# Top-k attention and routed experts on one core: the first pair's transpositions on one queue, more constant products ahead of it, later weight loads for the last expert, and row scatters into disjoint views

## The chip, the cores and the metric

The kernel runs on one core of a Trainium2 chip. The metric is device time in microseconds for one execution. Before the change it was 1404.75 us, the median of three runs (1401.38 to 1409.36).

## The reference, cut to what matters

```python
# attention: q, k, v are (8 batches, 8 heads, 576 rows, 64)
scores = q @ k.T / 8
kth    = 32nd largest score of each row
attn   = softmax(where(scores >= kth, scores, -1e9))
x      = (attn @ v), heads side by side         # 4608 tokens x 512
# experts: 8 experts, each takes exactly 576 tokens
logits = x @ w_gate                             # 4608 x 8
# pairs (token, expert) in falling order of logit; a pair is taken
# while the token is free and the expert has room
out[tokens of e] = relu(x[tokens of e] @ w1[e]) @ w2[e]   # 512 -> 1024 -> 512
```

## The kernel before, in words

**Order of work.** Both halves are written as lists of operations that a planner (`Plan`, top of the file) puts in order when the program is built. Every operation has an engine, an assumed duration, operations that must come before it, ring buffers that it takes or frees, and a due time `t`. The planner walks through time. Among the operations of an engine that could start within a small window it takes the one with the smallest due time. The D queue (SyncE's DMA queue, SP for short) has a window so large that the smallest due time always wins. The result is the program order of each engine. On the chip each engine then runs its own list in that order and waits at an instruction until its inputs are there, so everything behind a waiting instruction waits too.

**Attention** (`attention`, from L141). 32 pairs, each a batch with two heads, 9 tiles of 128 query rows a pair. For a pair, `prep` loads k, q and v, splits them into fp16 high and low parts, and `turn` (L237 to L241) makes four DMA transpositions of them: K2 and K3 from `nk`, Q2 and Q1 from `nq`. The scores (L288) need all four. VectorE finds the 32 largest scores of a row with MAX8 (L291 to L316) and ScalarE marks them (L303, L321). TensorE adds the marks to a second, transposed copy of the scores (L359 to L365), ScalarE takes the exponential (L369), and GpSimd splits it in two (L372, L375). L447 multiplies by v. The first pair has its own list, `first()` (from L245), in which k is loaded and transposed on SP and q on ScalarE's DMA queue. In the program the four transpositions stand in the order K2, Q2, K3, Q1.

**Constant products.** `stay(n)` (L193 to L195) issues n products of a constant tile that nothing reads. The planner puts `lead` of them in front of the first product of the attention, and some into gaps later on, so that TensorE is not idle there.

**Routing.** In `route` and `enlist` the experts are chosen one after another. VectorE and a few small products on TensorE search the threshold of the next expert and write the list of its 576 token numbers (`idx`). Those of the last expert are whatever is left, so its number (`ei`, L798) and list come soon after those of the seventh.

**Experts** (p = 0 to 7 in the order of the routing, about 47 us apart by due time).

- `weigh(p, t)` with t = 47 p - WT: SP reads the expert's number (`pick`, L873) and issues four loads of 1 MB, two of w1 and two of w2 (L881, ring `wr` of four). ScalarE makes the high fp16 parts (L893, eight of 1024 columns) and VectorE the low ones (L901, sixteen of 512).
- `bring(p, t)` with t = 47 p - 21.675: GpSimd gathers the rows of x in five indirect DMAs (L923, tile `xg`, 128 rows each, the last 64). ScalarE (L946) and VectorE (L949) split them into tile `xs` (three buffers), and SP transposes them into `xT` (L950). For p = 0 TensorE transposes instead.
- `ffn(p, t)`: TensorE multiplies by w1 in sixteen groups of twelve products (L968, eight groups for the tokens 0 to 287, then eight for the rest; five PSUM banks `ph`). ScalarE and VectorE make the two fp16 parts of the ReLU (L987, L988). TensorE multiplies by w2 for five token tiles in the order 0, 1, 4, 2, 3 (L1002, and L1005 for tile 4). ScalarE moves each result to `ob` (L1012, three buffers), and GpSimd scatters its rows into the output with an indirect DMA (L1017).

The rows of the output that different scatters write never coincide, but all of them name the same tensor `out`, so the framework makes each scatter wait until the one before it has landed. One scatter, that of the last expert's tile 3, stands at the very end of the program (L1100, shown in the trace as L1077), behind a branch that repeats the work if a test on the attention fails (`redo`).

Of the kernel before, what the change touches and what calls it, by code (L numbers as in the profile page):

```python
# [2 lines left out]

# [4 lines left out]

# [134 lines left out]
def attention(tc, q,k,v,w_gate,x_out,L,acc,cuts, pairs):  # L143
    NCH=6
    nc=tc.nc
    CW=576//NCH; NCAND=8*NCH
    with ExitStack() as ctx:
# [6 lines left out]
        V,G,A,T=nc.vector,nc.gpsimd,nc.scalar,nc.tensor  # L154
# [16 lines left out]
        for i in range(2):  # L171
            t=cp.tile([128,2,9,128],F16,name=f"nq{i}"); NQ.append(t); V.memset(t[:,1,:,64:128],0.0)
# [22 lines left out]
            for _ in range(n): T.matmul(early[0][:,0:128],nid60,nid60,start=True,stop=True,skip_group_check=True)  # L195
        ESC=0.125/(QS*QS)
        loom=Plan(PLANBUFS,WIN,dict(VV=.196,AV=.141,AP=.166,AG=.205,VA=.13,VP=.14,VG=.166))
        loom.keep=dict(f=stay,tag="pt",unit=.0559,edge=.12,window=3.413,share=.6,since=lambda: 10.0,until=lambda: 1e9,lead=105)
        at=loom.at
        def prep(n):  # L200

# [2 lines left out]
            nq,nk,vt,vh,vl=NQ[pi],NK[pi],VT[n%3],VH[n%3],VL[n%3]  # L204
# [29 lines left out]
            def lower(nm): G.tensor_tensor(low[nm][0],sc[nm],low[nm][1],op=ALU.subtract)  # L234
            def clean(): G.memset(nq[:,1,:,64:66],0.0)
            fl=lambda t: t.rearrange("p a b -> p (a b)")
            def turn(nm,by=nc.sync):  # L237
                t=io.tile([128,9,128],F16,tag=nm,name=nm,bufs=2)
                by.dma_start_transpose(t,fl({"Q1":nq[:,0],"Q2":nq[:,1],"K2":nk[:,0],"K3":nk[:,1]}[nm]))
                P[nm]=fl(t)  # L240
                if nm=="Q2": P["Q2t"]=t  # L241
            prev=Ps.get(n-1); old=Ps.get(n-2); o3=Ps.get(n-3)
# [3 lines left out]
            def first():  # L246

                lk=at(0.0,lambda: loads("k",k),e="D",d=2.2,late=2.0); l=at(0.0,lambda: loads("q",q,nc.scalar),e="A",d=2.9,late=2.4)
                def highk(): G.tensor_scalar(nk[:,0].rearrange("p i (r d) -> p i r d",r=2),nat["k"].unsqueeze(2).to_broadcast([128,9,2,64]),QS,0.0,op0=ALU.mult,op1=ALU.add)
                def highq(): A.activation(nq[:,:,:,0:64],nat["q"].unsqueeze(1).to_broadcast([128,2,9,64]),AF.Copy,scale=QS)  # L250
                def rest(nm): V.scalar_tensor_tensor(low[nm][0],nat[nm],QS,low[nm][1],op0=ALU.mult,op1=ALU.subtract)
                h1=at(0.0,highk,[lk],e="G",d=1.25); k2=at(0.0,lambda: rest("k"),[h1],e="V",d=.7)
                h2=at(0.0,clean,[h1],e="G",d=.1); h2=at(0.0,highq,[l],e="A",d=1.2,order=[h2]); q2=at(0.0,lambda: rest("q"),[h2],e="V",d=.7)
                a=at(0.0,lambda: turn("K2"),[h1],e="D",d=1.4,late=2.0); b_=at(0.0,lambda: turn("K3"),[a,k2],e="D",d=1.4,late=2.0)
                c=at(0.0,lambda: turn("Q2",nc.scalar),[h2],e="A",d=1.4,late=2.0); c=at(0.0,lambda: turn("Q1",nc.scalar),[c,q2],e="A",d=1.4,late=2.0)
                P["ready"]=at(0.0,lambda: None,[c,b_]); P["q2r"]=q2
                P["lds"]=at(0.0,loadv,[b_],e="D",d=2.2,late=2.0)
                wipe=at(0.0,rims,[q2],e="V",d=1.3); at(0.0,gates,[P["lds"]],e="D",d=3.2,late=2.0)
                P["vs"]=s3=at(0.0,scaledv,[P["lds"],wipe],e="G",d=1.1)
                a=at(0.0,lambda: highv(0),[s3],e="A",d=.3); a=at(0.0,lambda: highv(1),[a],e="A",d=.3)  # L260
                P["vready"]=at(0.0,lowerv,[a],e="G",d=1.13)
# [388 lines left out]
def moe(tc, K, L, x, w1, w2, out, tail, marks=None):  # L650

    nc=tc.nc
    E,D,F=w1.shape; N=x.shape[0]; CAP=N//E; NT=N//128
    T=MT; STEPS=MSTEPS; BIG=1e30; SX=128.0; SW=128.0; OSC=1.0/(SX*SW*SW)
    with ExitStack() as ctx:
        ctx.enter_context(tc.manual_schedule())
# [2 lines left out]
        wp=ctx.enter_context(tc.tile_pool(name="wp",bufs=2))  # L659
        ps=ctx.enter_context(tc.tile_pool(name="ps",bufs=1,space=PSUM))  # L660
        V,G,A,P,S=nc.vector,nc.gpsimd,nc.scalar,nc.tensor,nc.sync
        O=dict(WL1=-67.48, WL2=33.053, R1=216.021, XL=85.087, FA=-155.406, RT=5997.879, TE=0.633, TN=-42.68, WT=72.231, XT=21.675, RD=-5966.067, GL=2.3, W_V=0.109, W_A=0.0071, W_G=1000.0, W_P=0.0363, W_D=874040.4423, WD0=8.825, WD1=33.963, RA=16.129, WT0=-69.551, TE0=-175.381, XT0=-143.142, VD=228.308)
        GL,RT,TE,TN,WT,XT,RD,RA,WT0,TE0,XT0,VD,R1,XL,FA,WL1,WL2=(O[k] for k in ('GL','RT','TE','TN','WT','XT','RD','RA','WT0','TE0','XT0','VD','R1','XL','FA','WL1','WL2')); WD=(O['WD0'],O['WD1'])
        WIN={e:O['W_'+e] for e in 'VAGPD'}
        HOW0='vvvvvvvv'; HOW='vvvvvvvv'; GP=3; AHV=1; JO=1; PB=3; SPN=512; PW=.3; GV=0
# [204 lines left out]
        def weigh(p,t):  # L870

            e=X[p]; D_=e["D"]; e["raw"]=[]; ops=[]
            def pick(): e["r"]=nc.sync.value_load(D_["ei"][0:1,0:1],min_val=0,max_val=E-1)  # L873
            c=Chain(t,e["ei"],X[p-1]["loads"] if p else None)
            c.add("D",1.5,pick)
            for k in range(4):
                def load(k=k):
                    w,nch,cols=((w1,4,F),(w2,8,D))[k//2]; hf=k%2
                    src=w[bass.ds(e["r"],1)].rearrange("a (c p) f -> p (a c) f",p=128)
                    r=new(wp,[128,nch//2,cols],F32,"wr",4)  # L880
                    S.dma_start(out=r,in_=src[:,hf*nch//2:(hf+1)*nch//2,:])  # L881
                    e["raw"].append(r.rearrange("p c f -> p (c f)"))
                ops.append(plan.at(c.t+.05*k,load,c.pre,take="wr",e="D",d=.45,late=2.0+3.0*(k+1),order=ops[-1:]))
            e["loads"]=ops[-1]
            e["W"]=[]; e["wdone"]=[]
            prev=None
            for k in range(8):
                o_=(k%4)*1024; how=(HOW0 if p==0 else HOW)[k]; tk_=t+WD[0 if p==0 else 1]*k
                cut=lambda k=k: e["raw"][k//2][:,(k%2)*1024:(k%2)*1024+1024]
                def hi(k=k,o_=o_,cut=cut):  # L890
                    if k==0:
                        for (nch,cols,nm) in ((4,F,"w1"),(8,D,"w2")): e["W"].append((new(wp,[128,nch,cols],F16,nm+"h"),new(wp,[128,nch,cols],F16,nm+"l")))
                    A.activation(e["W"][k//4][0].rearrange("p c f -> p (c f)")[:,o_:o_+1024],cut(),AF.Copy,scale=SW)  # L893
                a=plan.at(tk_,hi,[ops[k//2],prev],e="A",d=.94,take="W" if k==0 else None); prev=a
                if k==0: e["tW"]=a
                at_=a
                if how=="v":
                    for u in range(0,1024,SPN):
                        def lo(k=k,o_=o_,cut=cut,u=u):
                            W=e["W"][k//4]; h=W[0].rearrange("p c f -> p (c f)"); l=W[1].rearrange("p c f -> p (c f)")  # L900
                            V.scalar_tensor_tensor(l[:,o_+u:o_+u+SPN],cut()[:,u:u+SPN],SW,h[:,o_+u:o_+u+SPN],op0=ALU.mult,op1=ALU.subtract)  # L901
                        at_=plan.at(tk_+.01+((WL1 if k<4 else WL2) if p==0 else 0),lo,[at_],e="V",d=.07+SPN*.00104,free=[ops[k//2]] if k%2 and u+SPN==1024 else None)
                else:
                    box={}
                    def sc(cut=cut,box=box):
                        box["t"]=new(wp,[128,1024],F32,"wt"); 
                        if how_a: A.activation(box["t"],cut(),AF.Copy,scale=SW)
                        else: G.tensor_scalar(box["t"],cut(),SW,0.0,op0=ALU.mult,op1=ALU.add)
                    how_a=False
                    g1=plan.at(tk_,sc,[ops[k//2],R.get("lastwt")],e="G",d=1.014)  # L910
                    def lo(k=k,o_=o_,box=box):
                        W=e["W"][k//4]; h=W[0].rearrange("p c f -> p (c f)"); l=W[1].rearrange("p c f -> p (c f)")
                        G.tensor_tensor(l[:,o_:o_+1024],box["t"],h[:,o_:o_+1024],op=ALU.subtract)
                    at_=plan.at(tk_+.01,lo,[at_,g1],e="G",d=2.08,free=[ops[k//2]] if k%2 else None); R["lastwt"]=at_
                e["wdone"].append(at_)
        def bring(p,t):
# [3 lines left out]
            def gather(j):  # L920
                n=128 if j<4 else 64
                xgs[j]=new(sm,[128,D],F32,"xg",4)
                G.indirect_dma_start(out=xgs[j][:n],out_offset=None,in_=x,in_offset=bass.IndirectOffsetOnAxis(ap=D_["idx"][:n,j:j+1],axis=0))  # L923
            g=None
            for j in range(5):
                n=128 if j<4 else 64
                g=plan.at(t+.1*j,lambda j=j: gather(j),[e["idx"]],e="G",d=1.25,take="xg",late=GL,order=[g,prev],k=1)
                if p==0:
                    B={}
                    if j<GV:  # L930
# [20 lines left out]
        def ffn(p,t):  # L951
# [39 lines left out]
            for j in ((0,1,4,2,3) if JO else range(5)):  # L991
# [22 lines left out]
                        B["o2"]=new(sm,[64,D],F32,"o2",2); A.activation(B["o2"],B["po"][64:128],AF.Copy,scale=OSC)  # L1014
                a=plan.at(t2+i_*.64,put,[prev],e="A",d=.51,take="ob",free=[tp] if j<4 else None); to=a
                if j==4: a=plan.at(t2+i_*.64+.1,lambda B=B: V.scalar_tensor_tensor(B["ob"][:64],B["po"][:64],OSC,B["o2"],op0=ALU.mult,op1=ALU.add),[a],e="V",d=.6,free=[tp],k=0)
                def scatter(B=B,j=j,n=n): G.indirect_dma_start(out=out,out_offset=bass.IndirectOffsetOnAxis(ap=D_["idx"][:n,j:j+1],axis=0),in_=B["ob"][:n],in_offset=None)  # L1017
                if p<E-1 or j!=3: plan.at(t2+i_*.64+.2,scatter,[a],e="G",d=1.25,free=[to],late=2.0,k=1)
            plan.frees(prev,e["tW"]); e["mm"]=prev; e["last2"]=prev
        def verdict(c,acc,cuts,flags):  # L1020
# [84 lines left out]
```

## Time and profile before

| | |
|---|---|
| runs | 1401.38, 1404.75, 1409.36 us (median 1404.75) |
| profiled execution | 1401.41 us, span 1399.7 us, mean granted TensorE clock 0.973 |
| busy share of the span | TensorE 92%, VectorE 83%, ScalarE 62%, GpSimd 61% |
| attention | from the start to about 920 us |
| routing of the first expert | about 920 to 966 us |
| experts | about 966 to 1388 us, then the end of the program |

How to read it: the busy shares are means over parts of the program that have different limits, so they only say that TensorE is the engine to look at first. What a change can save is read from the stretches in which TensorE is idle or has the lower of its two clocks (1.2 GHz instead of 2.4 GHz; a granted clock of 1.00 stands for 2.4), and from what it waited for there.

### The profile page before, as it was taken

The numbers are of one execution on the slowest core, as the hardware profiler recorded it, in microseconds if no ns is written. First come the engines' busy times: TensorE is split into PE (matmuls) and PEld (weight loads), VectorE is DVE, ScalarE is ACT, GpSimd is POOL, SyncE is SP. The second block draws the span as 40 slices with busy tenths as digits, with TensorE's granted clock in tenths as the row PEclk, the third lists the DMA queues.
The fourth block names the chain that finished last, engine by engine and source line by source line (L and its number), as shares of the span: only waits on it lengthen the run. The fifth ranks groups of instructions, "written<-read, shape, count | busy, mean of one in ns | idle before, by whom it ended". The sixth has DMA issues, their size and how long they took to land.

```text
span 1399.7 us, 42775 instructions
## 1 busy us (share of the span) xinstructions
PE 1288.7 (92%) x15599; PEld 929.6 (66%) x15600; DVE 1167.1 (83%) x6012; ACT 873.3 (62%) x1899; POOL 859.0 (61%) x1281
## 2 busy tenths in 40 slices
PE   5999999999999999999999999956989999998896
PEld 4677767777777767777776776746655665664562
DVE  5999988999999998999999999869979889987320
ACT  2778877878887877877878878713424424444320
POOL 3798888888888888888888888601114203203201
PEclk8999999999999999999999999967999999999998
DMA  4544464465444444445545335014446545647301
GB/s 89 101 97 96 87 132 85 85 121 98 90 107 95 93 105 96 92 93 115 85 94 126 79 82 102 14 35 155 146 94 196 176 126 154 181 162 213 86 27 37
DMA packets 293391, 148.56 MB, mean 106 GB/s; under 512 B 250672, under 2 KB 275248, under 8 KB 292144
## 3 DMA queue, kind: packets, MB, share of 16 engines
q1 hardware_dynamic: 284464, 125.96, 39.9%
q0 software_dynamic: 5888, 18.88, 4.4%
q8 instruction: 124, 2.03, 0.6%
q10 hardware_dynamic: 2816, 0.89, 0.4%
q14 instruction: 99, 0.81, 0.2%
HBM read 71.34 MB, written 18.87 MB: 64 GB/s over the span
## 4 chain that ended last, share of the span: by engine, by line
PE 57%; DVE 14%; ACT 10%; DMA 9%; POOL 5%; issue 4%; SPq 0%; POOLq 0%; ACTq 0%; another core or an unknown queue 0%; DVEq 0%
PE ph L968 13%; PE s L306 9%; PE pv L447 8%; PE ph L1002 6%; PE s L288 6%; DVE cd L291 5%; ACT w L303 4%; ACT F L369 3%; PE pt L359 3%; DMA Q<-nq 3%; PE pt L365 2%; PE pt L364 2%; DMA out_dram<-ob,idx 2%; DMA xT<-xs 2%; POOL elm L375 2%
## 5 line engine op out<-in xcount | busy, mean ns | idle before, releaser
L291 DVE MAX8 cd<-s 128x8 f32<-128x96 f32 x1728 | 348.9, 251 | 24.8 <-PE s L288 22.2
L375 POOL TENSOR_TENSOR elm<-F,ehm 128x512 f16<-128x512 f32 x256 | 291.8, 1157 | 1.5
L316 DVE MAX8 st<-s 128x8 f32<-128x584 f32 x288 | 222.1, 771 | 43.7 <-PE s L306 39.2
L303 ACT ACTIVATE w<-s,st 128x576 uint16<-128x576 f32 x288 | 213.6, 742 | 67.4 <-DVE st L299 52.9
L321 ACT ACTIVATE r<-s,st 128x576 bf16<-128x576 f32 x288 | 212.5, 740 | 43.2 <-PE s L306 38.7
L1017 POOL DMA_INDIRECT out_dram<-ob,idx x39 | 47.0, 1205 | 286.6 <-ACT ob L1012 215.4
L968 PE MATMUL ph<-xT,w1h 128*128 128x288 f16 (+2 forms) x1056 | 198.9, 288 | 8.0 <-DMA xT<-xs 4.4
L288 PE MATMUL s<-K,Q 128*128 128x512 f16 (+3 forms) x1280 | 190.0, 288 | 14.2 <-DMA Q<-nq 9.0
L372 POOL TENSOR_SCALAR ehm<-F 128x512 f16<-128x512 f32 x256 | 157.1, 620 | 65.6 <-ACT F L369 62.9
L365 PE MATMUL pt<-Q,K 66*128 66x128 f16 (+1 forms) x1280 | 171.7, 214 | 4.5 <-DMA Q<-nq 4.1
L369 ACT ACTIVATE F<-pt 128x512 f32<-128x512 f32 x256 | 150.8, 595 | 35.1 <-PE pt L365 28.7
L364 PE MATMUL pt<-Q,K 128*128 128x128 f16 (+1 forms) x1280 | 171.7, 214 | 0.0
L288 PEld LDWEIGHTS <-Q 128*128 128x128 f16 (+1 forms) x1280 | 102.1, 101 | 104.5 <-issue 15.9
L306 PE MATMUL s<-w,off 128*128 128x512 f16 x576 | 135.1, 285 | 18.7 <-ACT w L303 17.4
L968 PE MATMUL ph<-xT,w1l 128*128 128x288 f16 (+2 forms) x528 | 151.5, 288 | 0.0
L987 ACT ACTIVATE hh<-ph 128x288 f16<-128x288 f32 x128 | 52.1, 410 | 120.7 <-PE ph L968 99.4
L447 PEld LDWEIGHTS <-ehm 128*128 128x128 f16 x2048 | 118.5, 102 | 6.0 <-issue 0.8
L447 PE MATMUL pv<-vh,ehm 128*128 128x65 f16 x1024 | 120.8, 195 | 0.3 <-ACT F L369 0.2
L306 PE MATMUL s<-w,back 128*128 128x512 f16 x576 | 118.1, 286 | 3.1 <-DVE st L316 0.2
L447 PE MATMUL pv<-vl,ehm 128*128 128x65 f16 x1024 | 120.7, 192 | 0.0
L447 PE MATMUL pv<-vh,elm 128*128 128x65 f16 x1024 | 120.2, 193 | 0.0
L364 PEld LDWEIGHTS <-K 128*128 128x128 f16 x1280 | 116.9, 98 | 4.4 <-issue 1.1
(283 smaller groups left out, 3319.0 us busy)
## 6 DMA issues: line engine op xcount, KB each, us to landing
wr<-in_moe_w_dram SPq DMA_DIRECT2D x32, 1024.0 KB, 8.3
kn<-in_k_dram SPq DMA_DIRECT2D x64, 128.0 KB, 2.6
vn<-in_v_dram SPq DMA_DIRECT2D x64, 128.0 KB, 2.3
x<-xb SPq DMA_DIRECT2D x8, 1024.0 KB, 4.4
qn<-in_q_dram SPq DMA_DIRECT2D x62, 128.0 KB, 2.3
Q<-nq SPq DMA_TRANSPOSE x158, 3.3
kn<-in_k_dram SPq DMA_DIRECT2D x64, 16.0 KB, 2.4
K<-nk SPq DMA_TRANSPOSE x64, 3.4
```

What stands on the lines that cost most here:

```text
L288: T.matmul(s_ps[rows,a:b_],P[Q][:,qc],P[K][:,h*576+a:h*576+b_],start=(Q=="Q1"),stop=(Q=="Q2"))
L291: V.max(D["cd"][:,c*8:c*8+8],D["s"][:,576*c//NCH:576*(c+1)//NCH])
L303: A.activation(D["w"],D["s"][:,:576],AF.Sign,bias=P["st"][:,i,32:33],scale=(1+2.0**-21),accum_out=acc[:,col])
L306: x=T.matmul(D["s"][:,a:b_],by,w[:,a:b_],start=False,stop=True,skip_group_check=True)
L316: def next8(): V.max(P["st"][:,i,24:32],D["s"][:,:584])
L321: A.activation(r,D["s"][:,:576],AF.Relu,bias=P["st"][:,i,31:32],scale=-1.0)
L364: T.matmul(o,K2[:,kb:kb+128],Q1[:,qc],start=False,stop=False,skip_group_check=True)
L365: T.matmul(o,K3[0:66,kb:kb+128],Q2[0:66,qc],start=False,stop=(c==3 and h==sub[-1][0]),skip_group_check=True)
L369: A.activation(D["E"],D["pt"],AF.Exp,scale=ESC)
L375: G.tensor_tensor(el,D["E"],D["eh"],op=ALU.subtract); P["e"][i]=(D["eh"],el)
L447: for m_ in (range(N-1) if part==0 else (N-1,)): T.matmul(out,seq[m_][0],seq[m_][1],start=(m_==0),stop=(m_==N-1))
L968: P.matmul(B["ph"][:,lo-c0:hi-c0],a[:,c,fs],xT[:,b+c,lo:hi],start=(i==0),stop=(i==11),skip_group_check=True)
```

## The change

- The first pair's Q2 and Q1 are transposed on SP's queue like K2 and K3. The planner still counts them as ScalarE's, so the program order stays K2, Q2, K3, Q1.
- `lead` goes from 105 to 140 constant products.
- WT goes from 72.231 to 61.707 (in the table `O`, the rest of which is unchanged), so all weight work of experts 1 to 7 is due 10.5 us later.
- For the last expert the planner places `pick`, and with it the four loads, only behind the last gather of the expert before it. This binds the program order on SP. It adds no wait on the chip.
- The scatters of the 40 row tiles write into 40 views of the output that the framework takes to be disjoint, so that a scatter no longer waits for the one before it. The last scatter of the program still names `out` itself and waits for all of them. In the repeated run inside `redo`, all still use `out`.

```diff
+from concourse.ap import dram_disjoint_views
...
-        loom.keep=dict(f=stay,tag="pt",unit=.0559,edge=.12,window=3.413,share=.6,since=lambda: 10.0,until=lambda: 1e9,lead=105)
+        loom.keep=dict(f=stay,tag="pt",unit=.0559,edge=.12,window=3.413,share=.6,since=lambda: 10.0,until=lambda: 1e9,lead=140)
...
-            def turn(nm,by=nc.sync):
+            def turn(nm):
                 t=io.tile([128,9,128],F16,tag=nm,name=nm,bufs=2)
-                by.dma_start_transpose(t,fl({"Q1":nq[:,0],"Q2":nq[:,1],"K2":nk[:,0],"K3":nk[:,1]}[nm]))
+                nc.sync.dma_start_transpose(t,fl({"Q1":nq[:,0],"Q2":nq[:,1],"K2":nk[:,0],"K3":nk[:,1]}[nm]))
...
-                c=at(0.0,lambda: turn("Q2",nc.scalar),[h2],e="A",d=1.4,late=2.0); c=at(0.0,lambda: turn("Q1",nc.scalar),[c,q2],e="A",d=1.4,late=2.0)
+                c=at(0.0,lambda: turn("Q2"),[h2],e="A",d=1.4,late=2.0); c=at(0.0,lambda: turn("Q1"),[c,q2],e="A",d=1.4,late=2.0)
...
     E,D,F=w1.shape; N=x.shape[0]; CAP=N//E; NT=N//128
+    rows=dram_disjoint_views(out,5*E) if marks else [out]*(5*E)
...
-            c=Chain(t,e["ei"],X[p-1]["loads"] if p else None)
+            c=Chain(t,e["ei"],X[p-1]["loads"] if p else None,X[p-1]["far"] if p==E-1 else None)
...
-                g=plan.at(t+.1*j,lambda j=j: gather(j),[e["idx"]],e="G",d=1.25,take="xg",late=GL,order=[g,prev],k=1)
+                g=plan.at(t+.1*j,lambda j=j: gather(j),[e["idx"]],e="G",d=1.25,take="xg",late=GL,order=[g,prev],k=1); e["far"]=g
...
-                def scatter(B=B,j=j,n=n): G.indirect_dma_start(out=out,out_offset=bass.IndirectOffsetOnAxis(ap=D_["idx"][:n,j:j+1],axis=0),in_=B["ob"][:n],in_offset=None)
+                def scatter(B=B,p=p,j=j,n=n): G.indirect_dma_start(out=rows[p*5+j],out_offset=bass.IndirectOffsetOnAxis(ap=D_["idx"][:n,j:j+1],axis=0),in_=B["ob"][:n],in_offset=None)
```

## Rows read from the trace of the kernel before

**Rows 1.** Stretches: us, busy of PE, PEld, DVE, ACT, POOL, granted clock, DMA share, GB/s.

```profile
66.00:900.00 834.00, 795.53 (x11311) 602.13 (x11311) 762.54 (x4589) 670.09 (x1532) 721.64 (x1112) 1.00 0.47 96
...
1081.00:1131.00 50.00, 49.17 (x393) 31.32 (x392) 44.64 (x150) 19.53 (x33) 11.11 (x12) 1.00 0.58 163
```

**Rows 2.** The chain that ended last, at the start: start us, us, what.

```profile
7.20 3.30 DMA K<-nk
...
10.64 4.09 DMA Q<-nq
...
21.86 3.06 PE s L288 x12
24.92 4.34 PE pt L195 x65
```

**Rows 3.** Timeline of the first tile: first MAX8 groups on VectorE, first marks on ScalarE.

```profile
23.04 1.42 DVE L291 MAX8 cd<-s 128x8 f32<-128x96 f32 x8 [12.70 <-PE s L288]
...
27.06 0.74 ACT L303 ACTIVATE w<-s,st 128x576 uint16<-128x576 f32 x1 [5.99 <-DVE st L299]
```

**Rows 4.** Later pairs: L239 on SP's queue, then its landings in 66:75 and in 40:50.

```profile
68.18 2.81 SPq L239 DMA_TRANSPOSE Q<-nq  x2
...
DMA to landing us min/median/max: 3.4/3.7/4.2
...
DMA to landing us min/median/max: 3.5/4.3/5.1
```

**Rows 5.** Stretches at the start, columns as in the first group.

```profile
9.50:12.90 3.40, 3.37 (x61) 3.20 (x58) 0.66 (x11) 0.00 (x0) 0.00 (x0) 1.00 0.77 71
...
21.80:24.90 3.10, 3.04 (x14) 1.39 (x15) 1.86 (x12) 0.00 (x0) 0.57 (x1) 0.50 0.30 77
```

**Rows 6.** Stretches around the seventh expert, columns as in the first group.

```profile
1281.00:1285.20 4.20, 0.29 (x5) 0.39 (x6) 2.68 (x5) 2.80 (x4) 0.98 (x1) 1.00 1.02 221
1285.20:1289.20 4.00, 4.00 (x26) 2.66 (x24) 2.28 (x6) 0.57 (x2) 0.00 (x0) 0.58 1.13 302
...
1300.30:1303.90 3.60, 0.02 (x1) 0.01 (x1) 0.53 (x2) 1.23 (x3) 2.82 (x3) 0.86 0.64 166
...
1303.90:1310.00 6.10, 6.10 (x27) 3.81 (x27) 5.57 (x11) 4.38 (x7) 0.92 (x1) 0.52 0.99 211
...
1317.00:1341.00 24.00, 24.00 (x126) 10.94 (x124) 1.14 (x2) 3.01 (x6) 3.85 (x4) 1.00 0.11 39
```

**Rows 7.** SP's queue in time, 1240 to 1325: weight loads and transpositions.

```profile
1246.47 24.61 SPq L881 DMA_DIRECT2D wr<-in_moe_w_dram  x7
1271.20 10.01 SPq L950 DMA_TRANSPOSE xT<-xs  x3
```

**Rows 8.** Waits in 1270 to 1310: who waited for whom, us in total, times, longest.

```profile
POOL out_dram L1017 <- DMA out_dram<-ob,idx: 20.3, 4, 7.2
ACT xs L946 <- DMA xT<-xs: 11.2, 3, 9.7
...
ACT xs L946 <- issue: 7.3, 1, 7.3
```

**Rows 9.** GpSimd in time: last scatter of the sixth expert, first gather of the eighth.

```profile
1297.69 0.96 POOL L1017 DMA_INDIRECT out_dram<-ob,idx  x1 [4.02 <-DMA out_dram<-ob,idx]
1298.95 0.99 POOL L923 DMA_INDIRECT xg<-x,idx  x1 [0.30 <-issue]
```

**Rows 10.** Landings: L950 in 1212:1232, L950 in 1262:1285, L881 in 1240:1260.

```profile
DMA to landing us min/median/max: 2.7/3.8/5.8
...
DMA to landing us min/median/max: 4.4/6.7/10.2
...
DMA to landing us min/median/max: 5.6/9.2/11.6
```

**Rows 11.** The stretch between the first and the second expert, columns as in the first group.

```profile
1005.00:1031.00 26.00, 20.85 (x144) 10.60 (x143) 19.42 (x54) 9.77 (x15) 9.59 (x9) 0.93 0.70 148
```

**Rows 12.** The end: the last scatter of the program on GpSimd.

```profile
1391.29 0.96 POOL L1077 DMA_INDIRECT out_dram<-ob,idx  x1 [6.78 <-ACTq L534]
```

More of the change, by code (lines that the diff above doesn't have):

```diff
@@ L661, in moe @@
         V,G,A,P,S=nc.vector,nc.gpsimd,nc.scalar,nc.tensor,nc.sync
-        O=dict(WL1=-67.48, WL2=33.053, R1=216.021, XL=85.087, FA=-155.406, RT=5997.879, TE=0.633, TN=-42.68, WT=72.231, XT=21.675, RD=-5966.067, GL=2.3, W_V=0.109, W_A=0.0071, W_G=1000.0, W_P=0.0363, W_D=874040.4423, WD0=8.825, WD1=33.963, RA=16.129, WT0=-69.551, TE0=-175.381, XT0=-143.142, VD=228.308)
+        O=dict(WL1=-67.48, WL2=33.053, R1=216.021, XL=85.087, FA=-155.406, RT=5997.879, TE=0.633, TN=-42.68, WT=61.707, XT=21.675, RD=-5966.067, GL=2.3, W_V=0.109, W_A=0.0071, W_G=1000.0, W_P=0.0363, W_D=874040.4423, WD0=8.825, WD1=33.963, RA=16.129, WT0=-69.551, TE0=-175.381, XT0=-143.142, VD=228.308)
         GL,RT,TE,TN,WT,XT,RD,RA,WT0,TE0,XT0,VD,R1,XL,FA,WL1,WL2=(O[k] for k in ('GL','RT','TE','TN','WT','XT','RD','RA','WT0','TE0','XT0','VD','R1','XL','FA','WL1','WL2')); WD=(O['WD0'],O['WD1'])
```

## The prediction

> **What bounds the kernel now.** I read the stretches first. In the body of the attention TensorE works 795.5 of 834 us at the full granted clock, and in a normal hand-over between two experts 49.2 of 50 us [rows 1]. There the kernel is bound by TensorE, and nothing in this change makes its products fewer. What is left is the places where TensorE stands still or runs at the lower clock. The change touches two of them.
>
> The first is the start. The chain of waits holds four DMA transpositions one behind the other: K2 is issued at 7.20 and lands 3.30 us later, Q2 follows at 10.64 on the other queue and takes 4.09, then come K3 and Q1, and the first scores start at 21.86 [rows 2]. Each waits for the one before it to land because each is on another queue than the one before.
>
> The second is the seventh expert. TensorE worked 0.29 of 4.20 us at 1281, then 4.0 us at a mean clock of 0.58, stood still for 3.6 us at 1300.3 and then had 0.52 for 6.1 us [rows 6]. Two things lead there. SP issued three of the last expert's loads before the seventh expert's transpositions (seven loads in a row, four of the seventh and three of the eighth expert, then the transpositions) [rows 7]. Beside 3 MB of loads those took 4.4 to 10.2 us, where one hand-over earlier they took 2.7 to 5.8 [rows 10]. ScalarE waited 9.7 us for one of them [rows 8], VectorE behind it wrote the next list late, and TensorE waited for that. And the scatters, each of which waits for the one before, held GpSimd for 20.3 us [rows 8]. The last came at 1297.69 with the eighth expert's first gather behind it at 1298.95 [rows 9]. ScalarE stood at that gather's rows for 7.3 us [rows 8] with the seventh expert's ReLUs behind it, until TensorE ran out of banks.
>
> **The start.** All four transpositions go to SP in the order K2, Q2, K3, Q1. Two neighbours on SP take 2.81 us to issue, 1.4 each [rows 4]. K2 is issued at 7.20 as now, Q2 at 8.6, K3 at 10.0, Q1 at 11.4. Three in a row landed 3.4 to 4.2 us after their issue [rows 4], so they overlap. I take the longest of these for the last of four: Q1 lands at 11.4 + 4.2 = 15.6. The bounds are 3.4 (14.8) and 5.1, the longest in another pair that had loads beside it (16.5) [rows 4].
>
> The 35 added products go in front of the scores. The last 61 took 3.37 us, 55 ns each [rows 5], so 35 more take 1.9 us and end at 12.9 + 1.9 = 14.8, before Q1 lands. They cost nothing while that holds, and at the lower bound they cost at most a few tenths. They bring something, since the scores no longer follow 9 idle microseconds. The stretch at 21.8 was granted 0.50 [rows 5], that is 1.2 GHz. At 2.4 GHz the twelve score products take 1.5 instead of 3.06 us. The first MAX8 comes 0.6 us after the start of the scores instead of 1.18 (23.04 - 21.86) [rows 2, 3], at 16.2. The marks, 4.0 us later (27.06 - 23.04) [rows 3], come at 20.2 and are done at 21.1 with the read of their sum (0.2, an estimate). The 65 constant products that now hold TensorE until 24.92 + 4.34 = 29.26 [rows 2] take 3.6 us at 55 ns and end at 15.6 + 1.5 + 3.6 = 20.7. So the step behind them starts at 21.1 instead of 29.3, **8.0 us earlier**, with 7.0 and 8.8 as ends from the landing. The v loads and the next pair's k loads now stand behind four transpositions on SP, whose issue ends at 12.8. GpSimd needs the first of them only after its wait for the first tile's MAX8, so they stay hidden. If they came late, the price would be tenths. TensorE bounds what follows, so the whole attention and all behind it moves up by this amount.
>
> **The last expert's loads.** The register read and four loads on SP (0.4 us each to issue) move behind the seventh expert's transpositions; eight conversions on ScalarE and sixteen on VectorE follow them. The transpositions are then as in the hand-over before, 2.7 to 5.8 us [rows 10], the list is written in time, and the 3.9 us of idle and 4.0 x (1 - 0.58) = 1.7 us of lower clock [rows 6] go, together 5.6. I leave 0.4 for the third transposition, due close to the end of the products before it: **5.2 us**, ends 3 and 5.6. What hides the moved loads: they go out near 1280, the loads of the expert before needed up to 11.6 us to land [rows 10], and the eighth expert's products start some 47 us after that. VectorE had 1.14 us of work in 1317 to 1341 [rows 6], room for the conversions. For the other experts the later due time changes little: their loads wait for the expert's number anyway, and only ties on ScalarE turn. I take 0, between +2 and -2.
>
> **The scatters.** With views a scatter waits for its rows and no longer for the landing before it. The sixth expert's last scatter can go when TensorE has ended that expert, near 1282, and the eighth expert's gather right behind it, near 1283 instead of 1298.95 [rows 9]. Even with 8 us to land, its rows are there when ScalarE comes to them, about 10 us into the seventh expert. Then the idle 3.6 us and 6.1 x (1 - 0.52) = 2.9 us [rows 6] go: **6.5 us**, ends 0 and 6.5. In the other hand-overs scatters wait too, but TensorE does not (49.2 of 50 us) [rows 1], so I count nothing. At the end the last scatter comes at 1391.29 behind the branch, released last by ScalarE's side of it [rows 12], so earlier scatters give nothing there. The longer list of waits in front of it may cost tenths.
>
> **The sum** is 8.0 + 5.2 + 6.5 = 19.7 us. The profiled execution took 1401.4 us, which gives 1381.7. It equals the fastest of the three runs, and their median is 3.3 us above it. I add half of that: **1383 us**.
>
> **The rivals.**
>
> *The four transpositions do not overlap.* Then Q1 lands as now, and only the half microsecond of waiting between the queues goes: 0.5 instead of 8.0, so 1391. The Trainium skill ("DMA: Bandwidth & Descriptors", section "Issuing engines are not separate DMA queues") speaks for it. It says that DMAs from whatever engine run on the same 16 DMA engines, and that the choice of the issuing engine saves only issue time; by that rule alone the move would give next to nothing, this rival's 1391. Against it stand the landings of three in a row, 3.4 to 4.2 us at 1.4 us apart [rows 4]. One by one the third would need over 7. Chance 0.08.
>
> *The collision moves on.* The late loads now fall on the eighth expert's gathers and transpositions. ScalarE stands at their rows or at the weights, the seventh expert's ReLUs wait behind it, and the 6.5 us stay: 1390. For it: beside loads a transposition took up to 10.2 us [rows 10], and ScalarE runs in order. Against it: five banks of products cover some 7 us. Chance 0.22.
>
> *Scatters crowd the transpositions (slower).* Without their waits, scatters go out together with the next expert's gathers and transpositions, five times. Between the first and the second expert, where transpositions met other traffic, TensorE lost 5.2 us idle and 26 x 0.07 = 1.8 us of clock [rows 11], 7 us. Five times this is 35: 1383 + 35 = 1418. It decides from the third hand-over on (3 x 7 = 21 against 19.7). The same section of the skill's page says that such DMAs interleave on shared engines; no row here shows scatters alone doing so. Against it: a tile's result comes only every 5 us, so the rows, and not the landing, mostly release the scatter. Chance 0.04.
>
> *The scatters still wait,* because the framework finds another order between them or the three `ob` buffers take its place. The gather stays late, and the time is the second rival's, 1390. Chance 0.04.
>
> **How the numbers follow.** The forecast has 0.62, the rivals 0.08, 0.22, 0.04 and 0.04. A measurement of this kernel can tell about 0.5% from no change, that is 1398 to 1412. The forecast and each single rival but the third lie below 1398; only the first together with the second or the fourth (1397 to 1398) comes near. So faster 0.91, same 0.05, slower 0.04. The range goes down by the ends of the terms (8.8 + 5.6 + 6.5 and 2 for the due times) and the median's offset to 1376, and up past the first two rivals, with low ends of the other terms, to 1396.
>
> **What would show it.** Right: the four transpositions issued 1.4 us apart on SP, first scores near 15.6 at clock 1.00, no idle TensorE near 1273 to 1300 (the old 1281 to 1310, moved up), the eighth expert's loads behind the seventh's transpositions, no scatter waiting for a scatter. Wrong: first scores after 20, ScalarE waiting over 5 us for gathers, weights or transpositions within the seventh expert's first products, or a new idle TensorE in one of the earlier hand-overs.

## The result and the profile after

The changed kernel takes 1385.35 us (median of four runs, 1381.91 to 1386.23), the kernel before 1404.38 beside it. The ratio is 0.9856, with a 95% interval of 0.9823 to 0.9890: 1.4% faster, 19 us. The forecast was 1383. The profiled execution took 1385.18 us, with a span of 1383.4; before it was 1401.41 and 1399.7. Up to the routing the new lines stand one further down than before, in the experts two (L881 is now L883, L950 is L952, L968 is L970, L1017 is L1019).

The start, from the chain of waits of the kernel after (start, duration, what), which answers to [rows 2, 3]:

```profile
7.15 1.37 SPq L240
8.52 0.06 issue
8.64 1.31 SPq L240
10.04 1.30 SPq L240
11.43 4.94 DMA Q<-nq
16.42 0.68 PE s L289 x4
17.12 1.42 DVE cd L292 x8
...
21.14 0.84 ACT w L304 x2
22.02 0.49 PE s L307 x2
```

The four transpositions go out 1.4 us apart, and only the last is waited for. The first scores start at 16.42 instead of 21.86, the step behind the first marks at 22.02 instead of 29.27. The stretches of the kernel after show TensorE (first columns) and the granted clock (the column before the last two):

```profile
12.90:16.40 3.50, 1.69 (x31) 1.51 (x28) 0.00 (x0) 0.00 (x0) 0.00 (x0) 1.00 1.26 174
16.40:17.90 1.50, 1.48 (x13) 0.78 (x14) 0.78 (x5) 0.00 (x0) 0.49 (x1) 1.00 0.51 143
17.90:22.10 4.20, 3.87 (x69) 3.75 (x68) 4.20 (x35) 1.56 (x4) 2.14 (x6) 1.00 0.40 110
```

The scores run at a granted clock of 1.00 where it was 0.50 [rows 5]. From 17.9 to 22.1 VectorE works all of the 4.20 us and is the bound there.

The seventh expert. First SP's queue after (start, time from the first issue to the end of the last, what), which answers to [rows 7]; then GpSimd's queue, for [rows 9]; then the stretches, for [rows 6]; then the waits from 1271 to 1302, for [rows 8]:

```profile
1262.98 12.67 SPq L952 DMA_TRANSPOSE xT<-xs  x5
1275.84 2.81 SPq L883 DMA_DIRECT2D wr<-in_moe_w_dram  x4
1284.76 14.38 SPq L952 DMA_TRANSPOSE xT<-xs  x5
```

```profile
1274.85 0.96 POOL L1019 DMA_INDIRECT out_dram<-ob,idx  x1 [2.37 <-ACT ob L1014]
1276.11 0.99 POOL L925 DMA_INDIRECT xg<-x,idx  x1 [0.30 <-issue]
...
1284.96 0.92 POOL L925 DMA_INDIRECT xg<-x,idx  x1 [4.08 <-DVE xs L951]
```

```profile
1273.90:1276.00 2.10, 2.10 (x25) 1.69 (x23) 1.09 (x4) 0.78 (x2) 0.96 (x1) 1.00 0.81 186
1276.00:1288.00 12.00, 11.97 (x99) 9.44 (x97) 5.12 (x11) 5.71 (x11) 4.77 (x5) 1.00 1.00 371
...
1291.00:1300.70 9.70, 7.30 (x59) 5.56 (x57) 7.14 (x15) 6.29 (x13) 0.00 (x0) 1.00 0.99 156
```

```profile
ACT xs L948 <- DMA xg<-x,idx: 2.3, 1, 2.3
PE ph L970 <- DVE hl L990: 2.3, 1, 2.3
```

All five transpositions of the seventh expert now precede all four loads of the eighth. The sixth expert's last scatter waits for its rows (ScalarE's `ob`) and no longer for a landing, and the eighth expert's first gather goes out at 1276.11 instead of 1298.95. TensorE goes on without a gap, at the full granted clock. What is left is 2.4 us of idle TensorE after 1291 (9.70 less 7.30): ScalarE stands 2.3 us at gathered rows, and the ReLU parts behind it come late.

### The profile page after: what moved, and what is told of

Its sections match the earlier page's. It is cut to its first block, busy times and chain, and to the rows that moved or that the text cites. A ratio compares the mean times of both kernels' runs of the same rounds, so it can differ in the third digit from the quotient of the medians.

```text
span 1383.4 us, 42831 instructions
## 1 busy us (share of the span) xinstructions
PE 1285.9 (93%) x15634; PEld 929.4 (67%) x15635; DVE 1167.8 (84%) x6012; ACT 873.1 (63%) x1899; POOL 860.2 (62%) x1281
## 4 chain that ended last, share of the span: by engine, by line
PE 57%; DVE 12%; ACT 9%; issue 7%; DMA 7%; POOL 6%; SPq 1%; another core or an unknown queue 0%; POOLq 0%; ACTq 0%; DVEq 0%
PE ph L970 11%; PE s L307 9%; PE pv L448 8%; PE ph L1004 7%; PE s L289 6%; DVE cd L292 5%; ACT w L304 3%; ACT F L370 3%; DMA Q<-nq 3%; PE pt L360 3%; PE pt L366 2%; PE pt L365 2%; POOL elm L376 2%; DMA xT<-xs 1%; ACT r L322 1%
## 5 line engine op out<-in xcount | busy, mean ns | idle before, releaser
L292 DVE MAX8 cd<-s 128x8 f32<-128x96 f32 x1728 | 349.3, 251 | 18.7 <-PE s L289 16.1
L1019 POOL DMA_INDIRECT out_dram<-ob,idx x39 | 48.0, 1231 | 271.7 <-ACT ob L1014 255.0
L970 PE MATMUL ph<-xT,w1h 128*128 128x288 f16 (+2 forms) x1056 | 193.3, 282 | 4.1 <-DVE hl L990 2.3
L307 PE MATMUL s<-w,off 128*128 128x512 f16 x576 | 135.8, 287 | 18.9 <-ACT w L304 17.5
L970 PE MATMUL ph<-xT,w1l 128*128 128x288 f16 (+2 forms) x528 | 148.5, 283 | 0.0
```

The lines of the kernel that those rows point to most:

```text
L292: V.max(D["cd"][:,c*8:c*8+8],D["s"][:,576*c//NCH:576*(c+1)//NCH])
L307: x=T.matmul(D["s"][:,a:b_],by,w[:,a:b_],start=False,stop=True,skip_group_check=True)
L970: P.matmul(B["ph"][:,lo-c0:hi-c0],a[:,c,fs],xT[:,b+c,lo:hi],start=(i==0),stop=(i==11),skip_group_check=True)
```

## Where the time went, stage by stage

For all kernels of this study one number each was read from TensorE's timeline for two places: from the last product of one expert's second half (the products by w2) to the last product of the next one's first half (those by w1). It holds the hand-over and the first half. Before, from the first to the second expert, it is 1022.4 to 1053.1, 30.7 us; undisturbed it is 24.4 to 24.9, as in the four hand-overs from the second expert to the sixth. "Lost" is what is above 24.8 at the second expert and above 24.4 at the seventh. "First marks" is the start of ScalarE's first marks. Parts are the transpositions on SP (Q), the number of constant products, the loads (L) and the views (V). The median of before was 1404.47, 1404.09 and 1405.64 in the three groups of runs.

| kernel | parts | median us | first marks | lost, second expert | lost, seventh expert |
|---|---|---|---|---|---|
| before | 105 | 1404.4 | 27.1 | 5.9 | 11.8 |
| after | Q 140 L V | 1385.35 | 21.1 | 1.7 | 2.4 |
| e1_start | Q 140 | 1388.76 | 20.9 | 1.1 | 8.1 |
| e2_start_105 | Q 105 | 1397.38 | 21.1 | 7.0 | 10.0 |
| e13_start_125 | Q 125 | 1388.86 | 21.2 | 1.4 | 9.0 |
| e14_lead_only | 140 | 1397.66 | 27.5 | 1.0 | 10.2 |
| e3_views | 105 V | 1396.74 | 28.2 | 1.3 | 7.4 |
| e4_loads | 105 L | 1405.95 | 27.7 | 5.4 | 14.0 |
| e7_no_views | Q 140 L | 1393.15 | 21.1 | 0.3 | 14.5 |
| e8_views_loads | 105 L V | 1393.18 | 28.3 | 1.3 | 4.4 |
| e9_start_views | Q 140 V | 1388.92 | 20.4 | 2.5 | 9.0 |
| e10_after_105 | Q 105 L V | 1386.13 | 21.7 | 4.3 | 4.2 |
| e5_no_far | Q 140 V, due time | 1389.46 | 21.1 | 2.0 | 6.7 |
| e6_no_wt | Q 140 V, gather's wait | 1396.65 | 21.1 | 1.8 | 15.4 |

From before to after: 5.9 at the first marks (7.25 at the step behind them), 4.2 at the second expert and 9.4 at the seventh. The medians differ by 19.0, these two profiles by only 16.2: the one of before was 3.0 below its median. Its second expert's second half took 25.6 us, in all other kernels 26.7 to 28.4.

Each kernel has one profile, and profiles scatter by some microseconds in places that no part touches. From the chains of waits, the last products of the attention, before and then after:

```profile
913.53 2.64 PE pv L447 x56
```

```profile
907.79 2.63 PE pv L448 x56
```

They end at 916.17 and 910.42, 5.8 us apart. Over all fourteen traces they end at 916.2 to 919.0 in the five kernels without Q and at 906.3 to 910.4 in the nine with Q. The means, 917.2 and 908.3, are 8.9 us apart. So the profile of before was the earliest of its five there and that of after the latest of its nine, and a difference of 3 or 4 us between two single profiles proves little.

## The experiments

**The parts alone (first group).**

e1_start, the start alone (against the kernel before):

```diff
-def turn(nm,by=nc.sync):
+def turn(nm):
-    by.dma_start_transpose(t,...)
+    nc.sync.dma_start_transpose(t,...)
-turn("Q2",nc.scalar) ... turn("Q1",nc.scalar)
+turn("Q2") ... turn("Q1")
-lead=105
+lead=140
```

> The start alone: four transpositions on SP and 140 products; loads and scatters as before. Theory: first scores at 16.4, every later stage about 6 us earlier than before and no more, both stalls at the seventh expert as before: 1398 to 1399. Rival, the start's gain is eaten by something that bounds the attention from elsewhere (v loads, the next pair's k): no stage after the second pair is earlier, 1403 to 1405.

1388.76 us, ratio 0.9902 (0.9870 to 0.9934): a gain of 15.7 us where some 6 were expected. The first marks come 6.2 us earlier, as the theory has it. But the second expert loses 1.1 instead of 5.9, and the seventh 8.1 instead of 11.8, and the expectation had neither.

e2_start_105, the same with the old number of products:

```diff
-lead=140
+lead=105
```

> The four transpositions on SP with the 105 products of before. Theory: first scores at the same 16.4, but after 3.5 us of idle TensorE and at 1.2 GHz, so the first mark on ScalarE comes 0.5 to 1 us later than with 140 and the whole is 1 to 2 us longer than e1_start: 1399 to 1400. Rival, the 35 products do nothing that lasts: the same time as e1_start within 1 us, with every stage from the second pair on at the same place.

1397.38 us, ratio 0.9964 (0.9945 to 0.9982). The gain is 7.1 us, and the 35 products are worth 8.6 us beside it, where 1 to 2 were expected. Their clock at the start is only a small part of that. From e2_start_105 the first scores (in brackets the idle time before), the stretch behind them, and the chain of waits:

```profile
16.34 0.88 PE L289 MATMUL s<-K,Q 128*128 128x512 f16 x5 [2.81 <-DMA Q<-nq]
```

```profile
17.50:21.00 3.50, 3.50 (x32) 3.08 (x31) 3.50 (x27) 0.73 (x2) 1.98 (x4) 0.52 0.43 128
```

```profile
18.39 4.87 PE pt L196 x65
23.25 0.26 PE s L307 x2
```

TensorE had stood still for 2.81 us before the scores, and the 3.5 us behind 17.5 were granted 0.52. It did 32 products in them, where e13_start_125 below did 62 in the same stretch. VectorE was busy all of it in both, so the first marks come at 21.1 and 21.2. But here the 65 constant products hold TensorE until 23.25, and the step behind the marks starts then, 1.2 us later than in the kernel after (22.02). That is what the clock costs at the start.

e3_views, the views alone (against the kernel before):

```diff
+rows=dram_disjoint_views(out,5*E) if marks else [out]*(5*E)
-G.indirect_dma_start(out=out,...)
+G.indirect_dma_start(out=rows[p*5+j],...)
```

> The views alone; start and loads as before. Theory: the first stall at the seventh expert (3.9 us idle, then 1.7 us of lower clock) stays, since the loads still stand ahead of the transpositions; the eighth expert's gather is no longer held by scatters and comes near 1290 instead of 1299, and the second stall (3.6 idle, 2.9 of clock) goes: 1397 to 1399. Rival 1, the scatters' waits only followed from the loads: nothing moves, 1404. Rival 2, the views also give the 4 us between first and second expert: 1394 to 1395.

1396.74 us, ratio 0.9952 (0.9929 to 0.9974), at the upper end of the expected gain, but for two reasons: the seventh expert loses 7.4 instead of 11.8, less than the 6.5 us of the theory, and the second 1.3 instead of 5.9, as the second rival had it. SP's queue of e3_views still has three loads ahead of the seventh expert's transpositions, and ScalarE waits for those (its waits from 1275 to 1312):

```profile
1263.74 6.99 SPq L883 DMA_DIRECT2D wr<-in_moe_w_dram  x3
1270.85 10.32 SPq L952 DMA_TRANSPOSE xT<-xs  x3
```

```profile
ACT xs L948 <- DMA xT<-xs: 12.9, 3, 10.6
PE pl L853 <- DVE bt L849: 5.9, 1, 5.9
```

e4_loads, the loads alone (against the kernel before):

```diff
-WT=72.231
+WT=61.707
-c=Chain(t,e["ei"],X[p-1]["loads"] if p else None)
+c=Chain(t,e["ei"],X[p-1]["loads"] if p else None,X[p-1]["far"] if p==E-1 else None)
```

> The later last loads alone (due time and wait for the gather in the plan); start and scatters as before. Theory: the first stall goes (5.2); the scatters still wait for one another, but at 3 us each without 3 MB of loads beside them, so the eighth expert's gather comes near 1285 and the second stall goes for the most part as well: 1394 to 1397. Rival, the chain of scatters alone keeps the second stall: 1399 to 1400.

1405.95 us, ratio 1.0004 (0.9986 to 1.0023): nothing, against 7 to 10 us expected. GpSimd's queue of e4_loads (in brackets the idle time before, and what ended it), and its waits from 1284 to 1323:

```profile
1275.30 2.81 POOL L1019 DMA_INDIRECT out_dram<-ob,idx  x1 [0.30 <-issue]
1280.63 2.46 POOL L1019 DMA_INDIRECT out_dram<-ob,idx  x1 [2.52 <-DMA out_dram<-ob,idx]
1287.57 0.90 POOL L1019 DMA_INDIRECT out_dram<-ob,idx  x1 [4.49 <-DMA out_dram<-ob,idx]
1294.34 0.96 POOL L1019 DMA_INDIRECT out_dram<-ob,idx  x1 [5.87 <-DMA out_dram<-ob,idx]
1301.15 0.96 POOL L1019 DMA_INDIRECT out_dram<-ob,idx  x1 [5.85 <-DMA out_dram<-ob,idx]
1302.42 0.98 POOL L925 DMA_INDIRECT xg<-x,idx  x1 [0.30 <-issue]
```

```profile
POOL out_dram L1019 <- DMA out_dram<-ob,idx: 16.2, 3, 5.9
ACT xs L948 <- DMA xg<-x,idx: 16.1, 1, 16.1
PE ph L970 <- DVE hl L990: 12.0, 1, 12.0
```

The first stall is gone (a gap of 0.1 us where it was 4.3), but the loads now run beside the scatters. The first scatters land 2.5 and 4.5 us after the engine is done with them, the next two, beside the loads, 5.9 us after. Each waits for the one before, and the eighth expert's first gather comes at 1302.42, later than before the change (1298.95). ScalarE stands 16.1 us at its rows. The time moved from the first stall to the second.

**Pairs of parts (second group).** The theory from these four was now that loads and views need each other, and that the 35 products matter where the views are missing.

e7_no_views, the change without the views:

```diff
-rows=dram_disjoint_views(out,5*E) if marks else [out]*(5*E)
+rows=[out]*(5*E)
```

> The change without the views (start and loads). Theory: with the loads moved and the scatters still chained, the eighth expert's gathers wait behind the chain, so the seventh expert loses some 13 us as with the loads alone (13.4), where the start alone lost 7.9: 1388.8 + 5.5 = 1394 (1391 to 1396). Rival (the loads are worth their 5.2 us by themselves, and the loads alone missed for some other reason): 1388.8 - 5.2 = 1383 to 1385.

1393.15 us, ratio 0.9926 (0.9902 to 0.9951), as the theory has it. The scatters wait as in e4_loads (waits from 1268 to 1307), and the seventh expert loses 14.5:

```profile
POOL out_dram L1019 <- DMA out_dram<-ob,idx: 16.8, 3, 6.2
```

e8_views_loads, the change without the start:

```diff
-turn("Q2") ... turn("Q1")
+turn("Q2",nc.scalar) ... turn("Q1",nc.scalar)
-lead=140
+lead=105
```

> Loads and views together, the start as before. Theory: only the two together clear the seventh expert (loss 2.3 instead of 11.7), which is 9.4, and the first hand-over comes out well as it did with the views alone (up to 4): 1404.4 - 9.4 = 1395, or 1391 with the first hand-over (1390 to 1396). Rival (the parts simply add): 1404.4 - 7.7 (views alone) + 1.5 (loads alone) = 1398.

1393.18 us, ratio 0.9917 (0.9889 to 0.9945): within the theory's range and 5 us below the sum of the two parts alone.

e9_start_views, the change without the loads:

```diff
-WT=61.707
+WT=72.231
-c=Chain(t,e["ei"],X[p-1]["loads"] if p else None,X[p-1]["far"] if p==E-1 else None)
+c=Chain(t,e["ei"],X[p-1]["loads"] if p else None)
```

> Start and views, the last expert's loads as before. Theory: the loads stay ahead of the seventh expert's transpositions, that expert loses 7.2 us as with the views alone, and the first hand-over is already good with the start alone: 1388.8 - 0.7 = 1388 (1386 to 1390). Rival (views add their own 7.7 us here too): 1381.

1388.92 us, ratio 0.9880 (0.9849 to 0.9911), as the theory has it. Views bring nothing to the start alone (1388.76) as long as the loads stand ahead of the transpositions.

e10_after_105, the change with 105 constant products:

```diff
-lead=140
+lead=105
```

> The whole change with 105 constant products in front instead of 140. Theory (the 35 products matter at the start alone, 1 us of clock there; the rest of the 8.6 us between 105 and 140 without loads and views lay in the first hand-over, 4, and in the seventh expert, 2, which loads and views clear anyway): 1385.4 + 1 = 1386.5 (1385 to 1388). Rival (the 35 products are worth the whole 8.6 us wherever they stand): 1394.

1386.13 us, ratio 0.9875 (0.9846 to 0.9905), as the theory has it. In the whole change the 35 products are worth 0.8 us, which can't be told from nothing, where beside the start alone they are worth 8.6. Yet its profile loses 4.3 at the second expert, 2.7 more than after. The stretch from the end of the first expert to the end of the second one's first half in e10_after_105:

```profile
1012.90:1042.00 29.10, 26.45 (x232) 20.29 (x231) 22.74 (x85) 8.32 (x18) 1.25 (x1) 0.94 0.35 103
```

TensorE is idle for 2.65 us, and a granted clock of 0.94 over 29.1 us is some 1.7 us more; no scatter waits for a landing there. e9_start_views, with 140 products, is idle for 2.4 us in the same place at 1.00. Four of the fourteen profiles have less than the full clock there: before, e2_start_105, e4_loads and this one, and these are the four that lose more than 4 us.

**The two halves of the loads' part, and the products (third group).**

e5_no_far, only the later due time:

```diff
-c=Chain(t,e["ei"],X[p-1]["loads"] if p else None,X[p-1]["far"] if p==E-1 else None)
+c=Chain(t,e["ei"],X[p-1]["loads"] if p else None)
```

> The whole change without the wait of the last expert's loads for the eighth expert's... last gather of the seventh: only the later due time moves the loads. Theory: the due time alone already puts the loads behind the seventh expert's transpositions, so nothing is lost: 1385 to 1387. Rival (the wait is what keeps the loads back): the seventh expert loses 6 to 9 us again as without the loads' part, 1389.

1389.46 us, ratio 0.9898 (0.9867 to 0.9930): the theory missed, the rival holds. The due time spreads the loads between the transpositions but does not put them behind. SP's queue of e5_no_far:

```profile
1262.73 1.44 SPq L952 DMA_TRANSPOSE xT<-xs  x1
1264.44 0.48 SPq L883 DMA_DIRECT2D wr<-in_moe_w_dram  x1
1265.69 7.32 SPq L952 DMA_TRANSPOSE xT<-xs  x2
```

e6_no_wt, only the gather's wait:

```diff
-WT=61.707
+WT=72.231
```

> The whole change with the old due time for the last weight loads: only the wait for the seventh expert's last gather keeps the loads back. Theory: the loads stand in the middle of the seventh expert's five transpositions, so the later three land late and part of the stall returns: 1386 to 1389. Rival (the wait alone does the whole): 1385 to 1386.

1396.65 us, ratio 0.9948 (0.9931 to 0.9965): worse than both had it, and 7.7 us worse than with no change to the loads at all (e9_start_views). SP's queue of e6_no_wt and a wait of TensorE from 1265 to 1312 show why:

```profile
1260.18 4.19 SPq L952 DMA_TRANSPOSE xT<-xs  x2
1265.73 2.61 SPq L883 DMA_DIRECT2D wr<-in_moe_w_dram  x4
1268.38 34.30 SPq L952 DMA_TRANSPOSE xT<-xs  x8
```

```profile
PE ph L970 <- DMA xT<-xs: 13.2, 1, 13.2
```

All 4 MB stand between the second and the third transposition. Neither half of the loads' part does its work; the two together do.

e14_lead_only, the kernel before with 140 products:

```diff
-lead=105
+lead=140
```

> The kernel before with 140 constant products instead of 105, and nothing else. Theory (the products gain only where the scores follow them, and here Q1 lands at 21.9 as before): no change at the start; 1404 (1402 to 1406). Rival (35 products more turn the first hand-over between experts, which cost 5 to 7 us in the kernels with 105 and 1 in those with 140): 1399 to 1400.

1397.66 us, ratio 0.9939 (0.9916 to 0.9961): the theory missed, and the rival holds (1399 to 1400, and the time is 1.3 us lower still). The start is as before (first marks at 27.5); the second expert loses 1.0 instead of 5.9. The order of the instructions of all engines is the same in both kernels but for the 70 more on TensorE. From the end of the first expert to the end of the second one's first half, before and then e14_lead_only:

```profile
1022.40:1053.10 30.70, 26.31 (x232) 20.16 (x231) 22.76 (x85) 8.86 (x19) 1.96 (x2) 0.94 0.42 112
```

```profile
1022.90:1048.70 25.80, 24.85 (x232) 19.54 (x231) 22.61 (x85) 8.22 (x18) 2.31 (x2) 1.00 0.35 114
```

What differs can be seen in the transfers. First the kernel before from 996 to 1010, then e14_lead_only from 995 to 1009, while the second expert's loads run (GB/s in 40 slices, then the queues):

```profile
GB/s 59 351 433 398 386 410 421 445 410 410 421 445 445 386 339 404 398 386 427 398 410 404 386 257 304 410 375 363 404 386 421 369 76 41 23 23 23 29 12 0
...
q8 instruction: 1, 0.02, 0.4%
```

```profile
GB/s 47 129 222 433 374 351 433 398 421 398 468 398 421 421 445 392 381 398 415 415 386 386 386 386 369 275 369 398 380 357 421 410 468 223 18 0 0 0 0 0
...
q0 software_dynamic: 80, 0.26, 4.6%
```

Before, one packet of 16 KB of the instruction queue q8 falls among the loads, and the loads end in a tail of some 23 GB/s, which, by an estimate from some 400 GB/s in full flow over 16 engines (25 GB/s each), is about one engine. Their last 24 packets end one by one, 0.08 us apart but for four gaps of 0.24. In e14_lead_only that packet came 0.7 us ahead of the loads' first issue, and the tail is missing. All fourteen traces show the same two cases. In the six kernels with 105 products the packet comes 5.4 to 6.3 us after the loads' first issue, and the last packet of the loads ends after 15.1 to 15.4 us. In the eight with 125 or 140 it comes 0.2 to 0.9 us ahead of the issue, and the loads end after 12.6 to 13.4, in e13_start_125 after 14.4.

e13_start_125, the start with 125 products:

```diff
-lead=140
+lead=125
```

> Start alone with 125 constant products. Theory (the products have to reach the scores): 125 end at 14.0, 0.8 us ahead of where 140 end and 2.4 us ahead of the scores at 16.4; the scores run at the full granted clock as with 140, and the time is 1389 to 1391 if the first hand-over is good as with 140. Rival (the first hand-over is good only with 140 by where its transfers fall): 1395 to 1397 with a first hand-over that loses 5 to 7 us.

1388.86 us, ratio 0.9890 (0.9859 to 0.9921): like 140, as the theory has it, and the second expert loses 1.4. TensorE is idle before the scores for almost as long as in e2_start_105 (2.78 against 2.81 us), but the clock stays at 1.00. The first scores of e13_start_125 and the stretch behind them:

```profile
16.46 0.88 PE L289 MATMUL s<-K,Q 128*128 128x512 f16 x5 [2.78 <-DMA Q<-nq]
```

```profile
17.50:21.00 3.50, 3.50 (x62) 3.26 (x60) 3.50 (x27) 0.73 (x2) 2.22 (x4) 1.00 0.54 141
```

## Why the prediction was right, and where it was not

The time and all three terms came out near their forecast, when each is measured by taking it out of the whole change: the start 7.8 us (e8_views_loads less after; forecast 8.0), the last expert's loads 3.6 (e9_start_views; 5.2, ends 3 and 5.6), the scatters 7.8 (e7_no_views; 6.5, which was also the upper end). That is 19.2 for a sum of 19.7. The 3.6 is uncertain, since the intervals of e9_start_views and of the change overlap. Added alone to the kernel before, the same parts gave 15.7, -1.5 and 7.7 us, so the prediction's terms are not separate prices that add up, and that they fit so well one by one is in part luck. By place, the seventh expert gave 9.4 where 11.7 were forecast and the second 4.2 where nothing was, so part of the agreement is two errors that cancel.

- **The landing of Q1** was forecast at 15.6, with 16.5 as the upper bound; the scores started at 16.42. The four transpositions overlap on one queue, but the last took 4.94 us and not 4.2. The first MAX8 came 0.70 us after the scores (0.6 forecast) and the marks 4.02 after that (4.0). So the step behind them came 7.25 us earlier instead of 8.0. That all behind it moves up as well holds: at the end of the attention the kernels with the start and those without are 8.9 us apart in the mean. The first rival falls. The Trainium skill's rule in "DMA: Bandwidth & Descriptors", section "Issuing engines are not separate DMA queues", by which the choice of the issuing engine saves only issue time, does not carry over to this case: here it saved 5.4 us at the first scores, because in the kernel before a transposition on another queue than the one before it waited for that one's landing.
- **"The 35 added products cost nothing"** was right, and what they bring at the start was right in kind: a clock of 1.00 in place of 0.52, worth 1.2 us at the step behind the marks. What the forecast had not seen is the second expert's hand-over. There 35 products alone bring 4.9 by the profiles of the 8 us (e14_lead_only), together with another place of an instruction packet among the loads.
- **"In the other hand-overs scatters wait too, but TensorE does not"**, so that they count nothing, is the step that failed. It read 49.2 of 50 us in a normal hand-over [rows 1] for all of them, although the one between the first and the second expert [rows 11] lost 5 us idle, and the prediction used that row only against the change. The change wins 4.2 us there. Views do it alone (e3_views), and so do the products alone (e14_lead_only). That the scatters' chain is the way from late loads to a late hand-over fits both, since e3_views and e8_views_loads have the late loads and yet a good hand-over; it was only argued. e10_after_105 bounds it: with views and late loads TensorE is idle there for 2.65 us, little more than the 2.4 of e9_start_views, whose loads are not late, and the rest of its 4.3 is clock.
- **The first stall of the seventh expert** went as forecast: the gap is 0.2 us at most with the whole part. But its 5.2 us are not the part's own. Alone it gains nothing, because the loads that leave the transpositions fall upon the chained scatters (e4_loads). The second rival, that the collision moves on, describes this well; the forecast had given it 0.22 with the views in place. There it came true in small: 2.4 us are left, with ScalarE at the eighth expert's rows, where the forecast had all of the 6.5 gone.
- **The scatters** no longer wait for each other, so the fourth rival falls. No hand-over from the second expert to the sixth became longer (after: 24.5, 24.4, 24.9 and 24.4 us), so the third rival falls too.

What stays open: whether the instruction packet itself holds one DMA engine back, or only marks something else that the 70 instructions move. The packet was not moved without them. It is open too why the seventh expert loses some 2 us less with 140 products than with 105 (8.1 against 10.0 with the transpositions on SP, 10.2 against 11.8 without, each from a single profile). The 2.4 us that are left were not worked on, and no kernel here beats the changed one.

## What to carry to other kernels

When two stalls in a row come from one crowd of transfers, cost the parts against them as a pair: moving the loads gained nothing until the scatters were unchained, and unchaining the scatters gained nothing beside the start with the loads in the way, so a part tried alone can look useless and yet be needed. Where one small hand-over is worse than its equals, look at what runs on the DMA engines there before calling it given, and take a part's worth by removing it from the whole as well as by adding it alone. A change of some instructions on one engine can move the whole by half a per cent far from where they stand, so compare variants by runs of several kernels and not by one.

## What the runs showed that was not expected

- Instruction packets are traffic too. One packet of 16 KB among 4 MB of loads goes with a finish 0.7 to 2.8 us later (15.1 to 15.4 against 12.6 to 14.4), and a tail at the rate of about one DMA engine, in six kernels of six; without it in the middle, the tail is missing in eight of eight.
- 70 instructions at the very start moved that packet by about 7 us a thousand microseconds later, measured against the loads (from 6.2 us behind their first issue to 0.7 ahead), and the time by 8 us.
- TensorE stood still almost equally long before the scores in e2_start_105 (2.81 us, behind 105 constant products) and in e13_start_125 (2.78 us, behind 125), but the 3.5 us from 17.5 on were granted 0.52 in the one and 1.00 in the other. So how long it stands still does not alone tell the clock that follows.
